# Gated attention with two MLP blocks on one core: lighter attention for the first batch, five weight pieces staged at the start, the spatial gate evicted to SBUF

## The chip, the cores and the metric

The kernel runs on one core of one Trainium2 chip. The metric is the time of one execution in device microseconds (us); lower is better. Beside the plain times there is one execution recorded by the hardware profiler, with every instruction of every engine.

## What is computed

Three blocks follow each other for 4 batches of 768 tokens with width 384 (8 heads of 48). First a linear attention with a decay per channel:

```
for t in range(S):
    state = alpha[:, :, t, :, None] * state + np.einsum('bhd,bhe->bhde', k[:, :, t], v[:, :, t])
    y[:, :, t] = np.einsum('bhd,bhde->bhe', q[:, :, t], state)
```

Then two MLP blocks, each added to its input:

```
xn = (x - mu) / np.sqrt(var + 1e-06) * g_ln
ch = np.maximum(xn @ w_ch1, 0.0) @ w_ch2
...
h = x @ w_in                                  # then a tanh gelu
u, v = (h[..., :d_ff // 2], h[..., d_ff // 2:])
v_n = (v - mu) / np.sqrt(var + 1e-06) * g_ln
v_s = np.einsum('ts,bsd->btd', w_sg, v_n) + b_sg[None, :, None]
gated = u * v_s
return (x + gated @ w_out).astype(np.float32)
```

## The kernel before

**Tiles and stages.** The tokens are cut into 24 chunks of 128, six to a batch; attention goes chunk by chunk, with a state carried from one to the next. Two chunks make a group, of which there are 12. The MLP work of a group comes in units, one PSUM tile each: A is the first matmul of the channel MLP (tile `pg`, L633), B its second (L667), C the input matmul of the spatial MLP (`pgv` L707, `pgu` L732). Once per batch follow six D units, the spatial gate (`pgs`, L752), and six E units, the output matmul (`pgo`, L781). A single matrix product is made of three fp16 products, of a high and a low half of each factor, so every result is evicted twice: ScalarE writes the high half, VectorE (or GpSimd) the low half as the difference. The tiles `pg`, `pgv`, `pgu`, `pgs` and `pgo` share three PSUM buffers (tag "g").

**Attention of the first batch.** `whole = i < NF` marks the chunks 0 to 5. They are computed in fp32: alpha, q and k are transposed on TensorE (`pt`, L283), the products of the decays are eight scans on VectorE (`F` forward, `K` backward, L342), `F` is multiplied by q and `K` by k (L311). `kh` is `K` scaled by `rf`, one over the decay of the whole chunk, in four ScalarE instructions (L398), `ks` its transposed form (L406), `vs` a copy of v (L491). Scores go to `sc` (L436), are masked into `ss` (L444), and `psy` (L530, L536) is the chunk's result. Each chunk also has an input check: three squares summed on ScalarE (L500) and one maximum on VectorE (L502) into `st_in`. Chunks 6 to 23 work on fp16 halves, made by DMA transposes, and keep their own path. In the order of instructions and in the rows, `wk` stands for `F`, `K`, `ks`, `kh` and `ss` of chunks 1 and 3, which borrow another buffer.

**Weights.** The weights arrive as float64 words. A piece of 0.786 MB is loaded by SyncE's queue (SP) into one of three `stage` buffers, narrowed by one ScalarE instruction (`bits`, L129) and two VectorE instructions (L131, L133), and split into halves (L139 to L143, with TensorE, or L146 and L147). There are six pieces of w1, six of w2, and then w_in, w_sg and w_out. A list `ready` keeps the loads in order; each step of it narrows one piece and issues the load of the next.

**Order.** A table of times (`LATE, TC, D0, ...`) sets the order in which the steps are written; a scheduler then places every instruction in the in-order queue of its engine, by its own model of time. An engine executes its queue strictly in that order, and so does SP's queue, which issues all DMAs.

## Time and profile before

| | |
|---|---|
| median of 3 runs | 701.03 us (700.08 to 703.02) |
| the profiled execution's own time | 702.77 us |
| its span, first to last instruction | 701.0 us |
| TensorE (PE) busy | 650.6 us, 93% of the span |
| VectorE (DVE) | 465.3 us, 66% |
| ScalarE (ACT) | 435.5 us, 62% |
| GpSimd (POOL) | 181.0 us, 26% |

The profiled execution took 1.77 us more than its span, and 1.74 us more than the median of the plain runs. Shares are averages over stages of different kinds: the start of the kernel, while weights are still coming in, is not limited by the same engine as the middle.

### The profile page before, as it was taken

How to read it: one execution, taken by the hardware profiler on the slowest of the kernel's cores; microseconds unless marked ns; L12 is line 12 of the kernel's file. 1: busy time of each engine (PE TensorE's matmuls, PEld its weight loads, DVE VectorE, ACT ScalarE, POOL GpSimd, SP SyncE). 2: the span in 40 equal slices, each digit the busy share in tenths (PEclk: the TensorE clock that was granted, in tenths of full speed). 3: DMA queues.
4: the chain of work that ended last, by engine and by line, in shares of the span. 5: the costliest groups of instructions: out<-in, count | busy, mean ns of one | idle time of the engine just before them, and what ended most of it. 6: DMA issues, size and time to landing. Idle time of an engine off the chain costs nothing.

```text
span 701.0 us, 14486 instructions
## 1 busy us (share of the span) xinstructions
PE 650.6 (93%) x5658; PEld 489.4 (70%) x5658; DVE 465.3 (66%) x911; ACT 435.5 (62%) x871; POOL 181.0 (26%) x413
## 2 busy tenths in 40 slices
PE   5889998979999988989999978998989989999996
PEld 3757776767776875667777866676656877676783
DVE  7999675867476795557745896559655678333464
ACT  5887646676878488488755688488652656322230
POOL 2121101423516220433532220432404311201100
PEclk9999999999999999999999999999999999999999
DMA  9996679765475149367382159275140612110102
GB/s 227 226 260 167 204 178 169 155 113 95 91 121 80 28 86 190 84 108 116 59 115 56 30 100 183 76 127 85 40 86 15 88 34 58 34 24 12 36 1 72
DMA packets 228637, 70.64 MB, mean 101 GB/s; under 512 B 219472, under 2 KB 222544, under 8 KB 228560
## 3 DMA queue, kind: packets, MB, share of 16 engines
q1 hardware_dynamic: 228560, 69.63, 52.0%
q8 instruction: 46, 0.75, 0.5%
q14 instruction: 31, 0.25, 0.1%
HBM read 35.79 MB, written 4.72 MB: 58 GB/s over the span
## 4 chain that ended last, share of the span: by engine, by line
PE 43%; DVE 17%; ACT 17%; DMA 13%; issue 5%; POOL 3%; SPq 1%; ACTq 0%; DVEq 0%; POOLq 0%
PE pg L667 13%; PE pg L633 9%; PE pgs L752 6%; DMA stage<-stage 4%; PE pgu L732 4%; PE pgv L707 4%; PE pgo L781 3%; ACT stage L306 3%; DMA wgs<-wsp 2%; ACT junk L500 2%; ACT stage L290 2%; DMA inp<-in_alpha_dram 2%; DVE F L345 2%; DVE sc L449 2%; DMA inp<-in_q_dram 2%
## 5 line engine op out<-in xcount | busy, mean ns | idle before, releaser
L633 PE MATMUL pg<-xhT,w1s 128*128 128x256 f16 (+1 forms) x1404 | 151.5, 267 | 13.2 <-DVE hT L639 6.1
L633 PEld LDWEIGHTS <-w1s 128*128 128x128 f16 x1404 | 128.4, 99 | 31.2 <-issue 14.9
L667 PE MATMUL pg<-w2s,hT 128*128 128x384 f16 x864 | 143.7, 326 | 0.3 <-ACT vg L710 0.3
L667 PEld LDWEIGHTS <-hT 128*128 128x128 f16 x864 | 83.9, 98 | 54.3 <-issue 0.2
L752 PE MATMUL pgs<-wgs,vn 128*128 128x256 f16 x864 | 96.1, 273 | 1.5 <-ACT junk L766 1.5
L752 PEld LDWEIGHTS <-vn 128*128 128x128 f16 x864 | 84.0, 98 | 12.0 <-issue 1.7
L639 DVE SCALAR_TENSOR_TENSOR hT<-pg,hT 128x512 f16<-128x512 f32 (+1 forms) x74 | 49.3, 672 | 46.8 <-ACT hT L638 46.6
L306 ACT ACTIVATE stage<-stage 128x1024 uint16<-128x1024 uint16 x48 | 64.7, 1354 | 19.1 <-DMA stage<-stage 19.0
L290 ACT ACTIVATE stage<-inp 128x1024 uint16<-128x1024 uint16 x48 | 50.1, 1053 | 30.3 <-DVE K L345 18.4
L150 POOL TENSOR_TENSOR kh<-K,kh 128x512 f16<-128x512 f32 x17 | 20.4, 1199 | 129.2 <-ACT kh L414 129.2
L732 PE MATMUL pgu<-x2T,wis 128*128 128x256 f16 x432 | 50.7, 274 | 1.6 <-DVE hT L639 1.3
L707 PE MATMUL pgv<-wis,x2T 128*128 128x512 f16 x216 | 49.9, 381 | 1.5 <-DVE hT L639 1.2
L781 PE MATMUL pgo<-wos,uT 128*128 128x384 f16 x288 | 48.3, 326 | 1.2 <-DVE x L783 1.2
L732 PEld LDWEIGHTS <-wis 128*128 128x128 f16 x432 | 41.7, 98 | 9.1 <-DVE hT L639 2.2
L638 ACT ACTIVATE hT<-pg 128x512 f16<-128x512 f32 (+1 forms) x74 | 42.0, 577 | 9.7 <-PE pg L633 9.6
L500 ACT ACTIVATE junk<-inp 128x384 bf16<-128x384 f32 x72 | 37.2, 519 | 8.0 <-DMA inp<-in_q_dram 4.0
L781 PEld LDWEIGHTS <-uT 128*128 128x128 f16 x288 | 28.0, 98 | 19.9 <-issue 2.0
L150 POOL TENSOR_TENSOR qs<-F,qs 128x512 f16<-128x512 f32 x18 | 20.6, 1143 | 79.7 <-ACT qs L386 79.7
L707 PEld LDWEIGHTS <-x2T 128*128 128x128 f16 x216 | 20.9, 99 | 24.4 <-issue 2.1
L468 ACT ACTIVATE ss<-sc 128x512 f16<-128x512 f32 x36 | 21.1, 596 | 19.0 <-DVE sc L449 19.0
L759 DVE SCALAR_TENSOR_TENSOR pgs<-pgs,g2c,bbc 128x256 f32<-128x256 f32 x48 | 23.4, 487 | 11.3 <-PE pgs L752 10.6
L716 DVE TENSOR_SCALAR vg<-vg,mvv,rv 128x512 f32<-128x512 f32 x24 | 13.8, 579 | 24.4 <-POOL rv L246 23.9
(172 smaller groups left out, 1100.8 us busy)
## 6 DMA issues: line engine op xcount, KB each, us to landing
stage<-in_moe_w_ch_dram SPq DMA_DIRECT2D x24, 384.0 KB, 5.2
inp<-in_alpha_dram SPq DMA_DIRECT2D x24, 192.0 KB, 3.3
inp<-in_q_dram SPq DMA_DIRECT2D x24, 192.0 KB, 4.1
inp<-in_k_dram SPq DMA_DIRECT2D x24, 192.0 KB, 4.4
inp<-in_v_dram SPq DMA_DIRECT2D x24, 192.0 KB, 4.4
out_dram<-x SPq DMA_DIRECT2D x24, 192.0 KB, 2.4
stage<-in_moe_w_in_dram SPq DMA_DIRECT2D x4, 768.0 KB, 4.3
stage<-in_moe_w_sg_dram SPq DMA_DIRECT2D x6, 384.0 KB, 3.4
```

The lines of the kernel that those rows point to most:

```text
L150: (nc.vector if on_dve else nc.gpsimd).tensor_tensor(out=out, in0=in0, in1=in1, op=ALU.subtract)
L290: nc.scalar.activation(out=sp, in_=t[:, n].rearrange("p h d -> p (h d)").bitcast(U16) .rearrange("p (x w) -> p w x", w=2), func=AF.Copy)
L306: nc.scalar.activation(out=words[:, :, :, gap:], in_=tr, func=AF.Copy)
L500: nc.scalar.activation(out=junk()[:, 0:DM].rearrange("p (h d) -> p h d", h=H), in_=t[:, n, :, 0:D], func=AF.Square, accum_out=st_in[:, i, ...
L633: nc.tensor.matmul(out=pg[:, f, :], lhsT=w1s[:, a, kk, ff * P:(ff + 1) * P], rhs=xhT[j][:, r, kk, o], start=(n_ == 0), stop=(n_ == 3 * KD ...
L638: nc.scalar.activation(out=hi, in_=src, func=AF.Relu)
L639: last_dve[0] = nc.vector.scalar_tensor_tensor(out=lo, in0=src, scalar=0.0, in1=hi, op0=ALU.max, op1=ALU.subtract)
L667: nc.tensor.matmul(out=box[s], lhsT=hidden(a, f, s), rhs=w2s[:, r, f, :], start=(f == 0 and a == 0 and r == 0), stop=(f == KF - 1 and r == 1))
L707: nc.tensor.matmul(out=pg, lhsT=x2T[j][:, a, kk, o], rhs=wis[:, r, kk, DG:DI], start=(n_ == 0), stop=(n_ == 3 * KD - 1))
L732: nc.tensor.matmul(out=pg[:, f, :], lhsT=wis[:, a, kk, ff * P:(ff + 1) * P], rhs=x2T[j][:, r, kk, 0:N], start=(n_ == 0), stop=(n_ == 3 * K ...
L752: nc.tensor.matmul(out=pg[:, f, :], lhsT=vn[b * NCH + s][:, a, d * P:(d + 1) * P], rhs=wgs[th][:, r, s, :], start=(n_ == 0), stop=(n_ == 3 ...
L781: nc.tensor.matmul(out=pg, lhsT=gt[key][:, d // 2, a, d % 2, o], rhs=wos[:, r, d, :], start=(d == 0 and a == 0 and r == 0), stop=(d == KG ...
```

## The change

Five edits come together.

1. The first batch's chunks lose their input checks, their copy `vs` (v is read where it was loaded) and the four scalings into `kh`. In their place the backward scans come first, the chunk's decay is taken from them, and the forward scans start at one over that decay instead of at a constant, so that `F` carries the scaling. Four small VectorE instructions replace two. The scale of v moves into the mask and into the update of the state.
2. The state is decayed (GpSimd) ahead of `psy` instead of after it.
3. The first two weight pieces are staged in the two `hT` buffers, which nothing uses yet, so five pieces can be loaded before one is narrowed; five loads are outstanding instead of six.
4. The tiny load `g1c` goes ahead of the first chunk's inputs.
5. A D unit is evicted from PSUM by its two VectorE instructions into an SBUF tile `tm` (two buffers); the multiplication by u and the low half go from VectorE to GpSimd, and ScalarE reads `tm`.

```diff
+        if n_loads[0] <= 2: ring.tile([P, 1536], I32, tag="hT", bufs=2, name="stage")
...
+        def decay_state():
+            nc.gpsimd.tensor_tensor(out=state, in0=state, op=ALU.mult,
+                                    in1=st_fe[:, i, :].unsqueeze(2).to_broadcast([P, NP, 2 * D]))
...
-                decays(T["F"][:, p, :], T["a"][:, p, :], S_Q)
+        if whole:
+            @step
+            def _():
+                fe = st_fe[:, i, :]
+                r = T["rf"] = p2.tile([P, NP], F32, tag="rf", name="rf")
+                nc.vector.scalar_tensor_tensor(out=r, in0=T["K"][:, :, 0:1]..., in1=T["a"][:, :, 0:1]...)
+                nc.vector.tensor_scalar(out=fe, in0=r, scalar1=2.0 ** -101, scalar2=None, op0=ALU.max)
+                nc.vector.tensor_scalar(out=r, in0=fe, scalar1=1.0 / S_Q, scalar2=None, op0=ALU.mult)
+                nc.vector.reciprocal(out=r, in_=r)
+            for p in range(NP):
+                @step
+                def _(p=p):
+                    scan_F(p, T["rf"][:, p:p + 1])
...
-                for p in range(NP):
-                    nc.scalar.activation(out=T["kh"][:, p, :], in_=T["K"][:, p, :], func=AF.Copy,
-                                         scale=T["rf"][:, p:p + 1])
...
-                T["Kr"] = T["kh"]
+                T["Kr"] = T["K"]
...
-                nc.vector.tensor_tensor(out=m, in0=T["sc", e], in1=causal..., op=ALU.mult)
+                nc.vector.scalar_tensor_tensor(out=m, in0=T["sc", e], scalar=S_V, op0=ALU.mult, op1=ALU.mult,
+                                               in1=causal.unsqueeze(1).to_broadcast([P, NP, P]))
...
-                nc.scalar.activation(out=T["vs"], in_=t[:, 2, :, 0:D], func=AF.Copy, scale=S_V)
+        if whole:
+            T["vs"] = t[:, 2, :, 0:D]
...
-                    in_psum = b >= KG_
-                    tm = pg if in_psum else p1.tile([P, 2, U], F32, tag="tm", name="tm")
+                    tm = p2.tile([P, 2, U], F32, tag="tm", name="tm")
...
-                    nc.vector.tensor_tensor(out=tm, in0=tm, in1=uT[key][:, o, :], op=ALU.mult)
+                    nc.gpsimd.tensor_tensor(out=tm, in0=tm, in1=uT[key][:, o, :], op=ALU.mult)
                     nc.scalar.activation(out=gt[key][:, dp, 0], in_=tm, func=AF.Copy)
-                    low(in_psum, gt[key][:, dp, 1], tm, gt[key][:, dp, 0])
+                    nc.gpsimd.tensor_tensor(out=gt[key][:, dp, 1], in0=tm, in1=gt[key][:, dp, 0], op=ALU.subtract)
...
+        nc.sync.dma_start(out=g1c, in_=g1.rearrange("(k p) -> p k", p=P))
         load_chunk(0)
-        nc.sync.dma_start(out=g1c, in_=g1.rearrange("(k p) -> p k", p=P))
...
         load_chunk(1)
-        for _ in range(3):
+        for _ in range(2):
             wload()
```

The table of times is unchanged; the scheduler places the instructions anew. Three places matter.

The first is SP's queue at the start, which issues the loads (`inp_94` and `inp_95` are the two input buffers, `stage` from `w_ch` a half of a weight piece). Before:

```order
L231 DMA inp_94<-in_v_dram 128x8x48
L847 DMA g1c<-in_moe_g_ln_dram 128x3x1
L162 DMA stage<-in_moe_w_ch_dram 128x768 x6
L231 DMA inp_95<-in_alpha_dram 128x8x48
...
L231 DMA inp_95<-in_v_dram 128x8x48
L878 DMA g2c<-in_moe_g_ln_dram 128x4x1
L880 DMA bbc<-in_moe_b_sg_dram 128x768
L231 DMA inp_94<-in_alpha_dram 128x8x48
...
L231 DMA inp_94<-in_v_dram 128x8x48
L162 DMA stage<-in_moe_w_ch_dram 128x768 x2
```

Now:

```order
L889 DMA g1c<-in_moe_g_ln_dram 128x3x1
L236 DMA inp_94<-in_alpha_dram 128x8x48
...
L236 DMA inp_94<-in_v_dram 128x8x48
L167 DMA stage<-in_moe_w_ch_dram 128x768 x6
L236 DMA inp_95<-in_alpha_dram 128x8x48
...
L236 DMA inp_95<-in_v_dram 128x8x48
L167 DMA stage<-in_moe_w_ch_dram 128x768 x4
L921 DMA g2c<-in_moe_g_ln_dram 128x4x1
L923 DMA bbc<-in_moe_b_sg_dram 128x768
L236 DMA inp_94<-in_alpha_dram 128x8x48
```

The fourth and fifth weight piece moved ahead of the third chunk's inputs, and `g1c` ahead of the first chunk's.

The second is VectorE's queue where the first unit of the first group A is evicted (`hT<-pg`). Before:

```order
L370 TENSOR_SCALAR st_fe<-F 128x4
L586 SCALAR_TENSOR_TENSOR xsp<-psy,st_mv,xsp 128x384
L444 TENSOR_TENSOR wk<-sc,causal 128x512 x2
L373 RECIPROCAL rf<-st_fe 128x4
L311 TENSOR_TENSOR F<-pt,F 128x4x128
L502 TENSOR_REDUCE st_in<-inp_94 128x1
L567 TENSOR_TENSOR state<-psd,state 64x4x48 x2
L639 SCALAR_TENSOR_TENSOR hT<-pg,hT 128x384
```

Now:

```order
L316 TENSOR_TENSOR F<-pt,F 128x4x128
L316 TENSOR_TENSOR K<-pt,K 128x4x128
L474 SCALAR_TENSOR_TENSOR ss_856<-sc,causal 128x512
L474 SCALAR_TENSOR_TENSOR ss_857<-sc,causal 128x512
L351 SCALAR_TENSOR_TENSOR wk<-pt,consts 128x127 x4
L601 SCALAR_TENSOR_TENSOR state<-psd,state 64x4x48 x2
L378 SCALAR_TENSOR_TENSOR rf<-wk,pt 128x4
L381 TENSOR_SCALAR st_fe<-rf 128x4
L681 SCALAR_TENSOR_TENSOR hT<-pg,hT 128x384
```

(Rows of weight pieces in between are left out of both.) Before, the masks of chunk 3 (`wk<-sc`) and all scans of chunk 4 stood ahead of the first eviction; now only chunk 2's masks and chunk 3's backward scans do.

The third is GpSimd's queue at the first batch's D units. Before, it held only the attention's work there:

```order
L150 TENSOR_TENSOR kh<-K,kh 128x512
L304 MEMSET stage 128x5
L150 TENSOR_TENSOR qs<-F,qs 128x512
L573 TENSOR_TENSOR sp<-state,sp 128x384
L241 TENSOR_SCALAR ve<-st_mv 128x1
L559 TENSOR_TENSOR state<-state,st_fe 128x384
```

Now:

```order
L803 TENSOR_TENSOR tm<-tm,uT 128x512
L155 TENSOR_TENSOR qs<-F,qs 128x512
L615 TENSOR_TENSOR sp<-state,sp 128x384
L246 TENSOR_SCALAR ve<-st_mv 128x1
L805 TENSOR_TENSOR uT<-tm,uT 128x512
L345 TENSOR_TENSOR state<-state,st_fe 128x384
```

The two GpSimd instructions of each D unit (L803 and L805) are interleaved with the attention's, and one of them now stands ahead of `qs`.

## Rows read from the trace of the kernel before

**Rows 1.** The profile's page: span, and busy us of each engine.
```profile
span 701.0 us, 14486 instructions
PE 650.6 (93%) x5658; PEld 489.4 (70%) x5658; DVE 465.3 (66%) x911; ACT 435.5 (62%) x871; POOL 181.0 (26%) x413
```

**Rows 2.** Windows: stretch, length, busy us of PE, PEld, DVE, ACT, POOL; clock, DMA.
```profile
0.00:62.00 62.00, 49.26 (x313) 35.97 (x314) 54.18 (x127) 45.58 (x102) 14.47 (x41) 1.00 1.12 236
62.00:101.00 39.00, 39.00 (x394) 30.30 (x392) 29.01 (x53) 24.21 (x50) 2.81 (x8) 1.00 0.56 179
100.00:165.00 65.00, 57.66 (x474) 44.93 (x473) 42.87 (x86) 44.69 (x90) 18.69 (x40) 0.95 0.80 141
222.00:252.00 30.00, 30.00 (x344) 26.60 (x343) 21.04 (x40) 17.92 (x32) 6.97 (x14) 1.00 0.31 55
252.00:300.00 48.00, 42.66 (x363) 29.96 (x360) 31.16 (x57) 35.81 (x75) 12.69 (x31) 1.00 0.67 121
```

**Rows 3.** What PE waited for: us in total, times, longest.
```profile
PE pg L633 <- DVE hT L639: 6.1, 5, 2.5
PE pg L633 <- ACT junk L766: 5.4, 4, 1.9
PE pgs L752 <- ACT junk L766: 1.5, 1, 1.5
```

**Rows 4.** Groups of ACT by form, 0 to 130 us: busy, mean ns, idle before.
```profile
L500 ACT ACTIVATE junk<-inp 128x384 bf16<-128x384 f32 x18 | 9.3, 518 | 7.0 <-DMA inp<-in_q_dram 4.0 <-DMA wgs<-wsp 1.9 <-DMA inp<-in_k_dram 1.0
L398 ACT ACTIVATE kh<-K,rf 128x128 f32<-128x128 f32 x16 | 5.1, 398 | 2.1 <-DVE K L311 1.8 <-DVE st_mv L581 0.3
L500 ACT ACTIVATION_READ_ACCUMULATOR junk<-inp 128x1 f32 x18 | 3.4, 191 | 0.0
L491 ACT ACTIVATE vs<-inp 128x384 f32<-128x384 f32 x6 | 3.1, 510 | 0.6 <-DMA inp<-in_v_dram 0.6
L398 ACT ACTIVATE wk<-wk,rf 128x128 f32<-128x128 f32 x8 | 2.6, 397 | 0.0
```

**Rows 5.** What DVE and ACT waited for, 0 to 110 us.
```profile
DVE stage L131 <- ACT bits L129: 5.9, 7, 2.2
ACT bits L129 <- DMA stage<-in_moe_w_ch_dram: 4.9, 5, 2.2
```

**Rows 6.** Timeline of DVE: start, us, instruction, idle before.
```profile
7.82 0.14 DVE L370 TENSOR_SCALAR st_fe<-F 128x4 f32<-128x4 f32 x1
12.45 0.96 DVE L131 SCALAR_TENSOR_TENSOR stage<-stage,bits 128x768 int32<-128x768 int32 x1 [2.23 <-ACT bits L129]
23.44 0.55 DVE L502 TENSOR_REDUCE st_in<-inp 128x1 f32<-128x384 f32 x1
40.94 2.61 DVE L342 TENSOR_TENSOR_SCAN wk<-pt,consts 128x128 f32<-128x128 f32 x8
100.93 0.69 DVE L639 SCALAR_TENSOR_TENSOR hT<-pg,hT 128x512 f16<-128x512 f32 x1 [1.44 <-ACT hT L638]
```

**Rows 7.** Timeline of SP's queue: start, us, load.
```profile
3.55 1.13 SPq L847 DMA_DIRECT2D g1c<-in_moe_g_ln_dram  x1
```

**Rows 8.** Tile `pgs` and line L150: ns min/median/max, first to last start.
```profile
L759 DVE SCALAR_TENSOR_TENSOR pgs<-pgs,g2c,bbc x48: 472/492/494, 227.5 to 684.1; 128x256 f32<-128x256 f32 x48
L762 DVE TENSOR_TENSOR pgs<-pgs,uT x24: 690/700/700, 229.2 to 684.6; 128x512 f32<-128x512 f32 x24
L150 DVE TENSOR_TENSOR uT<-pgs,uT x24: 652/691/693, 231.7 to 686.0; 128x512 f16<-128x512 f32 x24
L150 POOL TENSOR_TENSOR vn<-vg,vn x19: 1151/1156/1547, 127.6 to 605.6; 128x512 f16<-128x512 f32 x19
```

**Rows 9.** Timeline after the first batch's last D unit.
```profile
252.95 0.47 DVE L759 SCALAR_TENSOR_TENSOR pgs<-pgs,g2c,bbc 128x256 f32<-128x256 f32 x1
254.79 0.58 ACT L766 ACTIVATE junk<-pgs 128x512 bf16<-128x512 f32 x1
```

**Rows 10.** The later chunks' forward scan on DVE: ns min/median/max.
```profile
L345 DVE TENSOR_TENSOR_SCAN F<-stage,reset x16: 1219/1224/1871, 167.5 to 570.1; 128x516 f32<-128x516 f32 x16
```

More of the change, by code (lines that the diff above doesn't have):

```diff
@@ L115, in stage_tile @@
         return ring.tile([P, 1536], I32, tag="stage", bufs=NST, name="stage")
+    n_loads = [0]
     def stage_load():
-        return stage_tile().rearrange("p (f w) -> p f w", w=2)
+        n_loads[0] += 1
+        t = ring.tile([P, 1536], I32, tag="hT", bufs=2, name="stage") if n_loads[0] <= 2 else stage_tile()
+        return t.rearrange("p (f w) -> p f w", w=2)
     low_bits = []
@@ L368, in _ @@
         def _():
+            if whole:
+                T["q"] = transposed(0)
+                return
             fe = st_fe[:, i, :]
@@ L380, in _ @@
             if whole:
-                work(["ks", "kh"], F16)
-                for n in ("ks", "kh"):
-                    T[n] = T[n].rearrange("p a n t -> p (a n t)").bitcast(F32).rearrange("p (n t) -> p n t", n=NP)
+                work(["ks"], F16)
+                T["ks"] = T["ks"].rearrange("p a n t -> p (a n t)").bitcast(F32).rearrange("p (n t) -> p n t", n=NP)
             else:
@@ L506, in _ @@
         def _():
+            if whole and c:
+                decay_state()
             psd = ps.tile([P, NP, 2 * D], F32, tag="t", bufs=2, name="psd")
@@ L521, in _ @@
                     first = False
+        if whole:
+            stats_step[i] = len(steps)
         @step
@@ L557, in _ @@
             if c < NCH - 1:
-                if c:
-                    nc.gpsimd.tensor_tensor(out=state, in0=state, op=ALU.mult,
-                                            in1=st_fe[:, i, :].unsqueeze(2).to_broadcast([P, NP, 2 * D]))
+                if c and not whole:
+                    decay_state()
                 for e in range(2):
@@ L563, in _ @@
                     m = slice(D * e, D * e + D)
-                    if c == 0:
+                    if whole and c:
+                        nc.vector.scalar_tensor_tensor(out=state[o, :, m], in0=T["psd"][o, :, m], scalar=S_V,
+                                                       in1=state[o, :, m], op0=ALU.mult, op1=ALU.add)
+                    elif whole:
+                        nc.vector.tensor_scalar(out=state[o, :, m], in0=T["psd"][o, :, m], scalar1=S_V, scalar2=None,
+                                                op0=ALU.mult)
+                    elif c == 0:
                         nc.vector.tensor_copy(out=state[o, :, m], in_=T["psd"][o, :, m])
```

45 lines of the change are left out of this document (26 added, 19 removed).

## The prediction

> **What bounds the kernel now.** I read the page first: the span is 701.0 us and TensorE is busy for 650.6 of it, so 50.4 us of TensorE's idle time is all that this change can win, unless it shortens TensorE's own work [rows 1]. It doesn't: the same matrix products remain. The windows say where that idle time lies [rows 2]. From 0 to 62 us TensorE works 49.26, so 12.7 us are open; VectorE works 54.18 there, ScalarE 45.58, and the DMA engines are full (share 1.12, 236 GB/s). From 62 to 101 TensorE has no gap at all. From 100 to 165 it idles 7.3, and the granted clock is 0.95 of the full 2.4 GHz, the lowest of these stretches. While the first batch's D units run (222 to 252) it has no gap either, and right behind them (252 to 300) it idles 5.3.
>
> The waits say for whom TensorE stands still [rows 3]. The A units' first matmuls (L633) wait 6.1 us for VectorE's `hT`, which is a PSUM buffer that comes free late, and 5.4 us for ScalarE's `junk` (L766), the last reader of a D unit's buffer; the D units themselves wait 1.5 us for the same. So two things are paid for: the ramp, where VectorE is late with evictions, and the three D stages that another batch follows, where the buffer is held too long.
>
> **The change, part by part.** The sum is made against the profiled execution's own time, 702.8 us; the median of the runs is 1.74 us lower.
>
> *ScalarE in the ramp.* It loses 18 squares (9.3) and their 18 accumulator reads (3.4), the scalings `kh` (5.1 and 2.6) and `vs` (3.1): 23.5 us [rows 4], most of it before 101 us. That is no gain by itself, since TensorE's waits of the ramp name VectorE. It counts where ScalarE holds VectorE up: 5.9 us on `bits`, of which ScalarE in turn spent 4.9 waiting for the piece to land [rows 5]. Only the difference, about 1 us, is ScalarE's own lateness.
>
> *VectorE in the ramp.* Six maxima of 0.55 go, 3.3 us; four small instructions of about 0.14 replace two in each of six chunks, 1.7 us more; net 1.6 us less [rows 6]. The other edits only change the form: the masks become a scalar_tensor_tensor that reads PSUM, and the state update another. The masks have no row in the new form; the nearest is `hT` at L639, also read from PSUM with 512 columns, at 0.69 us, and 0.70 for the plain tensor_tensor of that width [rows 6, 8]. I price them at nothing, with 1 us either way for twelve masks.
>
> *VectorE's order.* This is the larger part. The first unit of the first group A is now written before chunk 4's eight scans (2.61 us in one row of the timeline), chunk 3's masks and some statistics: about 10 us of VectorE's work stood ahead of that eviction and is behind it now [rows 6]. But ahead of the second group's first `hT` (100.93 us before [rows 6]) stands as much as before, less the 1.6. The 10 us are borrowed. They become a gain only as far as VectorE's own idle time is filled: it has 7.8 us of that up to 62, and 10.0 from there to 101 [rows 2]. Bounds: nothing, if VectorE's inputs still come at the same time (TensorE, which feeds it, has no gap from 62 to 101), and 8, about half of the 17.8 and most of TensorE's 12.7. I take **4**, nearer to the lower bound than to all of the idle time, as TensorE's waits on `hT` total 6.1 and not all of them lie here.
>
> *Five pieces at once, and `g1c`.* The fourth and fifth piece now pass chunk 2's inputs in SP's queue. The DMA engines are full, so two pieces of 0.786 MB at 236 GB/s push those inputs back by 6.7 us [rows 2], while ScalarE's wait for pieces is 4.9 in all [rows 5]: what the one wins the other may lose. Chunk 2's transposes are late if its inputs are. Net nothing; bounds 3 either way (a wait on pieces or a wait on chunk 2, whichever of VectorE's two sources is late next). `g1c` costs SP 1.13 us ahead of chunk 0's alpha [rows 7], at worst a loss of 1.1 at the very start. Against it stands that VectorE waited 2.23 us at 12.45 for the first `bits` [rows 6], which ScalarE, now without squares, can give sooner. Net nothing.
>
> *100 to 165 us.* The rest of the 23.5 us of ScalarE and the last of the borrowed order fall here, where ScalarE works 44.69 of 65 and VectorE 42.87 [rows 2]: neither is full. I take **1**, between 0 and 3 (3.3 is what the missing 5% of clock in 65 us is worth).
>
> *The D units.* VectorE loses 24 x (0.70 + 0.69) = 33 us. GpSimd gains 48 instructions; its nearest row is a subtraction of the same 128x512 at 1.156 us, between 1.151 and 1.547 [rows 8], so 55 us, 74 at the upper end. A unit thus gives it 2.31 us. The first batch's units follow each other every 5.1 us (first eviction 227.5, last 252.95, five steps [rows 8, 9]), and GpSimd's 6.97 busy us of 30 become 20.8 [rows 2]: it keeps up, if what it needs is there. What is bought is the buffer. Before, it came free when ScalarE's square was done, 254.79 + 0.58 = 255.37 for the last unit. Now it is free when the second eviction instruction has ended, 252.95 + 0.47 = 253.42, 2 us sooner [rows 9]. Three D stages are followed by other work, and the waits on `junk` are 5.4 + 1.5 = 6.9 us in all [rows 3]. VectorE's backlog adds to `hT`'s 6.1, of which I count half for these stages. Bounds: 2 (only the D-to-D waits and a part of the others) and 9 (6.9 plus most of 3). I take **5**, below 6.9, since a buffer that is free sooner hands part of the wait to VectorE, which is next in line. At the very end, where E needs the last low half, GpSimd is 2 x 1.156 - 1.39 = 0.9 us later than VectorE was: at most 0.9 lost.
>
> The page of the Trainium skill that bears on this speaks against the edit: the GPSIMD Engine Reference, section "Engine selection", sends elementwise work with two inputs to VectorE and calls GpSimd about twice as slow. This trace has 1.156 against 0.69 us, a ratio of 1.67. By the page's ratio the new work would be 48 x 1.39 = 67 us, 2.8 per unit; that is still under 5.1, so the sum is the same by either, and the page's warning counts for the third rival below. Its section "Specifications" adds that the two engines share SBUF interfaces. The row that bears on it here is the later chunks' forward scan, 1.224 us in the median and 1.871 at most [rows 10]; no row shows what ran beside it caused that.
>
> *Sum.* 4 + 1 + 5 = 10: 702.8 - 10 = 692.8 of a profiled execution, and 1.74 less, **691**, for the median.
>
> **Rivals.**
>
> *More than that.* VectorE's idle time in the ramp is filled to its bound (8), all waits of the D stages go (9), and the clock stays full from 100 to 165 (3, of 3.3). For it: ScalarE loses half of its 45.58 us of work in the ramp, and VectorE's waits on ScalarE chain on. Against it: TensorE had no gap from 62 to 101, so what it starts sooner must find its inputs sooner. 8 + 9 + 3 = 20, about 681; I centre it at 683. 0.22.
>
> *Given back.* The ramp is bound by VectorE's 54.18 of 62 us and by the DMA queue, and the 10 us are repaid at the second group: nothing. The D stages' waits become waits for `hT`, and 3 are left of the 5: 702.8 - 3 - 1.74 = 698, with 2 either way. For it: ahead of the second group's `hT` as much stands as before. 0.16.
>
> *Slower.* GpSimd's queue is strictly in order, and `qs`, `sp` and the state's decay of the next batch now stand between its two instructions of a D unit. The first of these waits for VectorE's evictions, which wait for a unit of TensorE. So an attention step can be late by the 2.31 us of a unit's work, and so can what TensorE does with it. With two chunks beside each of three D stages and the lateness once per chunk, two of these instructions each, that is 2 x 3 x 2.31 = 13.8 us against 10 won: 702.8 + 3.8 - 1.74 = 705. The point from which it decides is 10 / 6 = 1.7 us per chunk. For it: GpSimd goes from a quarter to two thirds of the stage. Against it: the attention's steps there are written well ahead of the chunk's end. 0.10.
>
> **How the numbers follow.** The forecast, 687 to 697, has 0.52: its lower end is the ramp's 6 with the D stages' 7 and the 1, its upper end 0 to 1 of the ramp with the D stages' 3 to 4. With 0.22 below, 0.16 at 698 and 0.10 at 705 these make 1. The range must leave out no more than 0.2: from 681, which cuts a little of the first rival (0.06), to 700, which leaves out the third and a little of the second (0.12). A measurement of this kernel can tell about 0.5%, 3.5 us, from no change, so faster is below 697.5: all of the forecast, the first rival, and a little of "given back", less a little of the forecast's upper end, 0.74. The same, up to 704.5, is the rest of "given back" and a part of the slower case's low end, 0.17. Slower has 0.09.
>
> **What would show it.** In the changed kernel's profile, TensorE should be idle some 4 us less in its first 62 to 101 us, the waits of L675 on `hT` should be nearer 2 than 6.1, and the waits on `junk` should be gone, as ScalarE no longer reads the buffer. GpSimd should be busy near 236 us and VectorE near 431. If chunk 2's inputs land late, VectorE or TensorE will name `inp` or `pt` in the first 40 us. If GpSimd is late, TensorE or ScalarE in the D stages will name `qs`, `sp` or `state`. The forecast is wrong if the scans or evictions on VectorE become much longer beside GpSimd's new work, if the two `tm` buffers fill (VectorE then names GpSimd's L805), or if the ramp's idle time only moves to the second group.

## The result and the profile after

The changed kernel takes 697.67 us (median of 8 runs, 695.06 to 699.68). The kernel before, run beside it, took 702.9 (8 runs), so the ratio is 0.9925, 95% interval 0.9904 to 0.9946: 5.3 us faster, where the forecast was about 10. The profiled execution took 697.87 us.

The page of the changed kernel, span and busy time, answers to [rows 1]:

```profile
span 696.1 us, 14452 instructions
PE 653.8 (94%) x5658; PEld 492.2 (71%) x5658; DVE 441.1 (63%) x870; ACT 416.6 (60%) x805; POOL 242.4 (35%) x462
```

TensorE idles 696.1 - 653.8 = 42.3 us, against 50.4. That is 8.1 us less, near the forecast's 10; but the same 5658 matmuls are busy 3.2 us longer, so only 4.9 us of the span are gone. Cut at the first D unit (223.4 us before, 221.7 after) and at the last matmul of E, the windows show where the 8.1 us were. Before:

```profile
0.00:223.40 223.40, 202.83 (x1661) 151.07 (x1662) 165.64 (x339) 157.37 (x318) 61.77 (x140) 0.98 0.78 161
223.40:694.90 471.50, 447.43 (x3999) 338.29 (x3997) 299.05 (x572) 278.14 (x554) 119.20 (x274) 1.00 0.41 73
```

After:

```profile
0.00:221.70 221.70, 202.84 (x1661) 151.68 (x1662) 167.74 (x346) 138.57 (x252) 59.96 (x142) 0.98 0.79 162
221.70:689.80 468.10, 450.59 (x3998) 340.52 (x3997) 272.72 (x524) 278.07 (x554) 182.49 (x322) 0.99 0.41 73
```

Ahead of the first D unit, the stretch called the ramp here, TensorE idles 18.9 us instead of 20.6; behind it, 17.5 instead of 24.1. The longer busy time lies behind it too.

The windows answer to [rows 2] (same stretches and columns):

```profile
0.00:62.00 62.00, 50.89 (x360) 37.32 (x361) 53.36 (x118) 38.05 (x67) 12.07 (x35) 1.00 1.07 236
62.00:101.00 39.00, 37.80 (x344) 29.44 (x342) 32.35 (x69) 18.19 (x32) 4.95 (x15) 1.00 0.83 204
100.00:165.00 65.00, 58.72 (x495) 45.92 (x493) 44.61 (x96) 40.15 (x76) 17.36 (x41) 0.95 0.70 132
222.00:252.00 30.00, 30.00 (x349) 27.03 (x347) 16.79 (x34) 18.53 (x38) 17.60 (x21) 1.00 0.35 57
252.00:300.00 48.00, 44.34 (x377) 30.52 (x375) 30.34 (x56) 35.93 (x72) 16.84 (x35) 0.96 0.69 123
```

Up to 101 us TensorE idles 12.3 us (11.1 + 1.2), and before 12.7. From 252 to 300 it idles 3.7 instead of 5.3, but the granted clock there is 0.96 and was 1.00.

What TensorE waited for (us in total, times, longest), beside [rows 3]:

```profile
PE pg L675 <- DVE hT L681: 9.1, 7, 2.6
PE pgo L822 <- DVE hT L681: 3.4, 3, 2.0
PE psd L546 <- ACT ks L436: 3.4, 1, 3.4
PE pgu L774 <- DVE hT L681: 0.9, 2, 0.5
```

The kernel before had two more rows on `hT`:

```profile
PE pgu L732 <- DVE hT L639: 1.3, 2, 0.8
PE pgv L707 <- DVE hT L639: 1.2, 2, 0.7
```

The waits on `junk` (6.9) are gone. The waits on `hT` grew from 8.6 in all to 13.4, and one long wait on `ks` is new.

Where the two places stand is told by the first and last start of a line's matmuls, for the A units (up to 300 us) and the first batch's D units. In the kernel before:

```profile
L633 PE MATMUL pg<-xhT,w1s x648: 217/272/418, 61.6 to 268.4; 128*128 128x256 f16 x108, 128*128 128x128 f16 x54
L752 PE MATMUL pgs<-wgs,vn x216: 270/273/282, 223.4 to 249.7; 128*128 128x256 f16 x108
```

In the changed kernel:

```profile
L675 PE MATMUL pg<-xhT,w1s x648: 217/272/283, 51.4 to 265.3; 128*128 128x256 f16 x108, 128*128 128x128 f16 x54
L794 PE MATMUL pgs<-wgs,vn x216: 269/273/282, 221.7 to 247.9; 128*128 128x256 f16 x108
```

The first group starts 10.2 us sooner; the first D unit only 1.7.

### The profile page after: what moved, and what is told of

Read it like the earlier page. It is cut to its first block, busy times and chain, and to the rows that moved or that the text cites. A ratio compares the mean times of both kernels' runs of the same rounds, so it can differ in the third digit from the quotient of the medians.

```text
span 696.1 us, 14452 instructions
## 1 busy us (share of the span) xinstructions
PE 653.8 (94%) x5658; PEld 492.2 (71%) x5658; DVE 441.1 (63%) x870; ACT 416.6 (60%) x805; POOL 242.4 (35%) x462
## 4 chain that ended last, share of the span: by engine, by line
PE 42%; DVE 21%; ACT 18%; DMA 11%; issue 4%; POOL 4%; SPq 1%; ACTq 0%; DVEq 0%
PE pg L709 11%; PE pg L675 7%; PE pgs L794 6%; PE pgo L822 5%; DMA stage<-stage 4%; PE pgv L749 4%; ACT stage L311 3%; PE pgu L774 3%; DMA inp<-in_alpha_dram 3%; ACT stage L295 2%; ACT junk L532 2%; DVE F L354 2%; DMA inp<-in_q_dram 2%; DVE sc L479 2%; DVE K L354 2%
## 5 line engine op out<-in xcount | busy, mean ns | idle before, releaser
L675 PE MATMUL pg<-xhT,w1s 128*128 128x256 f16 (+1 forms) x1404 | 152.5, 268 | 9.9 <-DVE hT L681 9.1
L675 PEld LDWEIGHTS <-w1s 128*128 128x128 f16 x1404 | 128.9, 99 | 28.5 <-issue 10.6
L311 ACT ACTIVATE stage<-stage 128x1024 uint16<-128x1024 uint16 x48 | 64.8, 1355 | 18.2 <-DMA stage<-stage 17.8
L822 PE MATMUL pgo<-wos,uT 128*128 128x384 f16 x288 | 50.2, 333 | 3.4 <-DVE hT L681 3.4
L749 PE MATMUL pgv<-wis,x2T 128*128 128x512 f16 x216 | 50.4, 384 | 0.1
L774 PEld LDWEIGHTS <-wis 128*128 128x128 f16 x432 | 42.3, 100 | 8.7 <-DVE hT L681 1.3
L800 DVE SCALAR_TENSOR_TENSOR tm<-pgs,g2c,bbc 128x256 f32<-128x256 f32 x48 | 20.9, 477 | 39.7 <-PE pgs L794 31.1
L822 PEld LDWEIGHTS <-uT 128*128 128x128 f16 x288 | 28.4, 100 | 22.8 <-issue 5.7
L155 POOL TENSOR_TENSOR qs<-F,qs 128x512 f16<-128x512 f32 x18 | 20.6, 1146 | 66.2 <-ACT qs L422 66.2
L246 POOL TENSOR_SCALAR ve<-mvv 128x1 f32<-128x1 f32 x24 | 5.3, 222 | 97.1 <-DVE mvv L756 95.9
L803 POOL TENSOR_TENSOR tm<-tm,uT 128x512 f32<-128x512 f32 x24 | 32.4, 1348 | 18.2 <-DVE tm L800 18.1
L804 ACT ACTIVATE uT<-tm 128x512 f16<-128x512 f32 x24 | 14.9, 623 | 36.1 <-POOL tm L803 36.1
```

Of the source, the lines that this page charges most:

```text
L155: (nc.vector if on_dve else nc.gpsimd).tensor_tensor(out=out, in0=in0, in1=in1, op=ALU.subtract)
L311: nc.scalar.activation(out=words[:, :, :, gap:], in_=tr, func=AF.Copy)
L675: nc.tensor.matmul(out=pg[:, f, :], lhsT=w1s[:, a, kk, ff * P:(ff + 1) * P], rhs=xhT[j][:, r, kk, o], start=(n_ == 0), stop=(n_ == 3 * KD ...
L749: nc.tensor.matmul(out=pg, lhsT=x2T[j][:, a, kk, o], rhs=wis[:, r, kk, DG:DI], start=(n_ == 0), stop=(n_ == 3 * KD - 1))
L774: nc.tensor.matmul(out=pg[:, f, :], lhsT=wis[:, a, kk, ff * P:(ff + 1) * P], rhs=x2T[j][:, r, kk, 0:N], start=(n_ == 0), stop=(n_ == 3 * K ...
L803: nc.gpsimd.tensor_tensor(out=tm, in0=tm, in1=uT[key][:, o, :], op=ALU.mult)
```

## The experiments

Each was compared with the kernel before on the same chip, in five rounds; its ratio is to that kernel, with a 95% interval. In each expectation, "theory" is the reading held likelier and "rival" the other. "First D unit" is the first start of the `pgs` matmuls in the profiled execution (223.4 before, 221.7 changed). It scatters: five complete kernels with all the ramp's edits (the changed one, `no_d`, `d_sbuf_dve`, `checks_dve`, `ks_dve`) have it between 221.0 and 223.8, so a difference of up to 3 us says nothing by itself. In `att_only` it is at 223.6, in `att_d` at 226.0 and in `stage_only` at 230.0, the last in the slowest of that kernel's 12 runs.

**The change in its parts.** `d_only` is the kernel before with edit 5 alone, `att_only` with edits 1 and 2, `stage_only` with 3 and 4, `no_d` with 1 to 4. The core of `d_only`'s edit:

```diff
-                    nc.vector.tensor_tensor(out=tm, in0=tm, in1=uT[key][:, o, :], op=ALU.mult)
+                    nc.gpsimd.tensor_tensor(out=tm, in0=tm, in1=uT[key][:, o, :], op=ALU.mult)
...
-                    low(in_psum, gt[key][:, dp, 1], tm, gt[key][:, dp, 0])
+                    nc.gpsimd.tensor_tensor(out=gt[key][:, dp, 1], in0=tm, in1=gt[key][:, dp, 0], op=ALU.subtract)
```

Expected of `d_only`:

> The kernel before with the D units' edit alone (eviction into tm by VectorE, multiplication and low half on GpSimd, tm with two buffers). Theory: TensorE's waits on junk (6.9 us before) go, a part comes back as waits on hT, idle falls by 4 to 6 us from 50.4, and the clock falls at one or two more places, which takes 1 to 3 us back: 2 to 4 us faster than before, ratio 0.994 to 0.997. Rival: the whole gain of the change (ratio 0.9925) is this edit's, 0.992 to 0.993, and the ramp's edits are worth nothing. Second rival: waits only change their name, 0.999 to 1.001.

Measured: 0.9932 (0.9911 to 0.9952). That is the first rival's range: the D edit alone gives nearly all of the change's gain. Its first D unit is at 223.9; the gain comes behind it. From there to E's last matmul, `d_only` takes 465.4 us and the kernel before 471.5. TensorE's idle time in that stretch parts the kernels more clearly than one length does: 22.1 to 24.6 us in the five kernels that keep a D unit in PSUM (before, `att_only`, `stage_only`, `no_d`, `no_wgs_before`), and 16.3 to 21.0 in the nine that evict it early and whose checks of chunks 6 to 23 are as in the changed kernel (some of these runs follow below).

Expected of `att_only`:

> The kernel before with the first batch's lighter attention alone (no checks, no copy of v, no scalings into kh, scans in the new order), six pieces staged as before, D units as before. Theory: VectorE has the same amount of work ahead of the second group's hT, so the earlier start of the first group is repaid: at most 2 us faster, ratio 0.997 to 1.000. Rival: the 23.5 us less of ScalarE's work is what made the changed kernel faster: 4 us or more, under 0.995.

Measured: 0.9987 (0.9974 to 1.0001). The lighter work of ScalarE, 23.5 us by the prediction's rows and 18.1 by its busy time (435.5 to 417.4; an accumulator's read overlaps its square), is worth about 1 us, 2 at most.

Expected of `stage_only`:

> The kernel before with five loads outstanding in five buffers, and g1c first; nothing else. Theory: nothing, 0.998 to 1.002, since DMA is full in the first 62 us and what a piece wins chunk 2's inputs lose. Rival: the weights were what the ramp waited for (ScalarE's 4.9 us on them): 3 us or more, under 0.996.

Measured: 1.0016 (1.0002 to 1.0029), no gain, which fits the DMA engines' share of 1.12 in [rows 2].

Expected of `no_d`:

> The changed kernel with the D units as they were (PSUM until the square is done, multiplication and low half on VectorE). Theory: keeps only the ramp's share, about 1.5 us: 0.996 to 0.999 of before, with TensorE idle some 49 us and first D unit at about 222 us, and the junk waits of 5 to 7 us back. Rival: the ramp's edits made the 5 us, 0.992 to 0.994.

Measured: 0.9972 (0.9954 to 0.999), 2 us, as the theory had it. In its trace the A units and the D units stand so:

```profile
L675 PE MATMUL pg<-xhT,w1s x648: 217/272/283, 51.3 to 267.9; 128*128 128x256 f16 x108, 128*128 128x128 f16 x54
L794 PE MATMUL pgs<-wgs,vn x216: 269/273/283, 222.9 to 249.2; 128*128 128x256 f16 x108
```

Ten us of lead at the first group again, and half a us of it left at the first D unit.

**The early start without the staging edit.** `att_d` has edits 1, 2 and 5.

```diff
-        if n_loads[0] <= 2: ring.tile([P, 1536], I32, tag="hT", bufs=2, name="stage")
...
-        for _ in range(2):
+        for _ in range(3):
             wload()
```

> The changed kernel without the staging edit and with g1c behind chunk 0's inputs, so the lighter attention and the D edit alone. The staging edit alone measured 1.0016. Theory: it is worth nothing or a little loss also here: 0.990 to 0.993 of before. Rival: it needs the lighter attention to pay (five pieces at once let the first group start at 51 us rather than 57), and without it 0.994 to 0.997.

Measured: 0.9932 (0.9909 to 0.9954). Staging and `g1c` don't matter here either.

**The D edit in two.** `d_sbuf_dve` leaves PSUM as early as the changed kernel, but VectorE multiplies and subtracts, in SBUF:

```diff
-                    nc.gpsimd.tensor_tensor(out=tm, in0=tm, in1=uT[key][:, o, :], op=ALU.mult)
+                    nc.vector.tensor_tensor(out=tm, in0=tm, in1=uT[key][:, o, :], op=ALU.mult)
```

(the subtraction likewise).

> The changed kernel with the multiplication and the low half of the D units back on VectorE, reading and writing the SBUF tile tm; PSUM is left as early as in the changed kernel. It parts the D edit in two. Theory: the early release of PSUM is what pays, so this one keeps most: 0.992 to 0.996, no waits on junk. Rival: it is VectorE's 33 us less that pay (hT comes sooner); then most of the D edit's gain goes: 0.996 to 0.999, and TensorE's waits on hT grow by several us.

Measured: 0.9925 (0.9895 to 0.9954), the changed kernel's own ratio. VectorE works 464.7 us in it, against 441.1 in the changed kernel. So the early release of the PSUM buffer pays; taking work from VectorE adds nothing that five rounds can tell.

GpSimd was not free of cost in the changed kernel either. In the third batch's D stage, both `tm` buffers are full, and VectorE waits for GpSimd to empty one, twice, while GpSimd waits for ScalarE's half:

```profile
553.64 1.16 POOL L805 TENSOR_TENSOR uT<-tm,uT 128x512 f16<-128x512 f32 x1 [2.30 <-ACT uT L804]
554.83 0.88 DVE L800 SCALAR_TENSOR_TENSOR tm<-pgs,g2c,bbc 128x256 f32<-128x256 f32 x2 [5.04 <-POOL uT L805]
559.28 0.88 DVE L800 SCALAR_TENSOR_TENSOR tm<-pgs,g2c,bbc 128x256 f32<-128x256 f32 x2 [3.57 <-POOL uT L805]
561.27 2.20 DVE L354 TENSOR_TENSOR_SCAN F<-stage,reset 128x516 f32<-128x516 f32 x1
562.34 2.19 POOL L803 TENSOR_TENSOR tm<-tm,uT 128x512 f32<-128x512 f32 x1
563.39 2.23 DVE L354 TENSOR_TENSOR_SCAN K<-stage,reset 128x516 f32<-128x516 f32 x1
564.56 0.63 ACT L804 ACTIVATE uT<-tm 128x512 f16<-128x512 f32 x1 [2.80 <-POOL tm L803]
566.34 0.20 PE L588 MATMUL psy<-vs,ss 128*128 128x48 f16 x1 [1.56 <-ACT ss L498]
569.11 0.98 PE L588 MATMUL psy<-vs,ss 128*128 128x48 f16 x20 [1.62 <-DVE ss L155]
```

VectorE's scans come behind these waits, and beside GpSimd's multiplication they take 2.2 us, where the median is 1.2; the multiplication takes 2.19, where its median is 1.27. ScalarE waits 2.80 us for that multiplication and evicts `ss` behind it. TensorE then waits 3.9 us on `ss` in three pieces (1.56, 0.70 and 1.62); in `d_only` the same three make 4.2, in `d_sbuf_dve` there are two of 1.39 and 0.42. So the work on GpSimd costs some 2 us of waits here; whether that is what it wins elsewhere, so that the two kernels measure the same, is not shown.

**ScalarE behind a D stage.** The changed kernel's ScalarE behind the first batch's last D unit, by start, length and idle time before it:

```profile
255.23 0.62 ACT L804 ACTIVATE uT<-tm 128x512 f16<-128x512 f32 x1
255.75 0.62 ACT L807 ACTIVATE junk<-tm 128x512 bf16<-128x512 f32 x1
256.27 0.19 ACT L807 ACTIVATION_READ_ACCUMULATOR junk<-tm 128x1 f32 x1
256.37 0.51 ACT L732 ACTIVATE junk<-x 128x384 bf16<-128x384 f32 x1
256.78 0.19 ACT L732 ACTIVATION_READ_ACCUMULATOR junk<-x 128x1 f32 x1
256.87 0.58 ACT L680 ACTIVATE hT<-pg 128x512 f16<-128x512 f32 x1
```

VectorE and TensorE there:

```profile
257.49 0.69 DVE L681 SCALAR_TENSOR_TENSOR hT<-pg,hT 128x512 f16<-128x512 f32 x1 [1.21 <-ACT hT L680]
258.23 2.13 PE L675 MATMUL pg<-xhT,w1s 128*128 128x256 f16 x18 [1.04 <-DVE hT L681]
267.51 12.89 PE L822 MATMUL pgo<-wos,uT 128*128 128x384 f16 x68 [1.96 <-DVE hT L681]
```

TensorE waits for VectorE's half of `hT`, VectorE for ScalarE's half, and ScalarE comes to it only after the last D unit's copy and square and one more square (L732). The buffer that came free sooner was filled by the next A unit, whose eviction stands in the same queue. `no_checks` takes load from that queue: it leaves the input checks of chunks 6 to 23 out.

```diff
-            @step
-            def _():
-                stats()
```

> The changed kernel without the input checks (three squares on ScalarE, one maximum on VectorE) of the chunks 6 to 23 as well; it leaves these checks out, as the changed kernel does for the chunks 0 to 5. Theory: behind a D stage TensorE waits on hT because ScalarE's queue is full (squares, copies for the transposes) and its hT copy comes late, so 38 us less of ScalarE's work take away a good part of the waits on hT (9.1 + 3.4 us) and some clock dips: 4 to 7 us faster than the changed kernel, 0.983 to 0.988 of before. Rival: these waits come from VectorE or GpSimd, or ScalarE's place in the order decides and not its load: within 2 us of the changed kernel, 0.990 to 0.994.

Measured: 0.9861 (0.9823 to 0.99), first D unit at 223.7. ScalarE works 392.0 us, VectorE 430.8 (the maxima are gone too), and TensorE idles 41.1. The theory's ratio, though the waits of L671 on `hT` are still 8.6 us. Of the 4.8 us of span that are gone against the changed kernel, 1.2 are idle time and 3.6 busy time of the same matmuls, at a clock of 0.989 instead of 0.984. What is shown is that this load costs time; that the gain comes by `hT` is not, nor which of the two engines it comes from. `checks_dve` computes the checks' squares on VectorE instead:

```diff
-                nc.scalar.activation(out=junk()[:, 0:DM]..., in_=t[:, n, :, 0:D],
-                                     func=AF.Square, accum_out=st_in[:, i, n:n + 1])
+                nc.vector.scalar_tensor_tensor(out=junk()[:, 0:DM]..., in0=t[:, n, :, 0:D], scalar=1.0,
+                                     in1=t[:, n, :, 0:D], op0=ALU.mult, op1=ALU.mult, accum_out=st_in[:, i, n:n + 1])
```

> The changed kernel with the squares of the input checks of chunks 6 to 23 on VectorE (three scalar_tensor_tensor with accumulated sums per chunk) in place of ScalarE; all checks are computed. Theory: behind D it is ScalarE's load that counts, and VectorE has room since the D edit; 54 squares of about 0.6 us are 35 us for VectorE, which then works as long as before the change. Most of the 4.5 us that leaving the checks out gave stays: 0.986 to 0.990 of before. Rival: VectorE writes the last half of hT, its new work comes ahead of that as ScalarE's did, and nothing is won or up to 4 us lost: 0.992 to 0.998.

Measured: 0.9923 (0.9894 to 0.9952), the rival: nothing won. VectorE works 469.9 us, and TensorE waits 10.8 us on `hT` at L675 and 5.0 at L822. So moving the squares off ScalarE is not enough: on VectorE, which writes the other half of `hT`, they cost about as much.

**The clock.** In windows of 1 us, the kernel before shows three stretches of some 3.4 us at the lower level (0.5 of 2.4 GHz, 1.2 GHz), ahead of its end, and the changed kernel five, one of them twice as long. Each comes right behind one of TensorE's long waits: 2.01, 2.16 and 2.53 us before; 3.42, 1.96, 2.60, 2.42, and 1.56, 0.70 and 1.62 shortly one after the other, after the change. Not every long wait is followed by one: those of 2.54 and 2.70 us in the first 10 us of the changed kernel are not, nor is one of 1.91 us on `junk` in the kernel before (at 411.76). Windows of the changed kernel around the first:

```profile
117.00:122.00 5.00, 4.87 (x46) 3.59 (x44) 2.44 (x4) 1.08 (x1) 0.64 (x2) 1.00 1.28 197
122.00:125.00 3.00, 0.00 (x0) 0.00 (x0) 2.12 (x3) 2.52 (x4) 1.54 (x5) 0.97 0.60 50
125.00:131.00 6.00, 5.70 (x26) 4.65 (x27) 3.75 (x8) 5.29 (x12) 2.30 (x7) 0.50 0.70 134
```

After 3 us without a matmul, TensorE is busy for 6 us at half the clock. Over the 8 runs of the changed kernel the clock lies between 0.978 and 0.989 and the spans between 697.8 and 693.2, with a correlation of -0.95. In other kernels time and clock go together less: -0.63 over the 92 runs of the kernel before beside the experiments, 0.07 over the 12 of `no_d`. TensorE's busy time does follow the clock: in the profiled executions of the 14 kernels with the same 5658 matmuls it goes from 649.1 us (`att_only`, clock 0.995) to 657.5 (`wgs_scalar`, 0.976), with a correlation of -0.95. The two profiled executions lie further apart than their kernels do: 0.992 before and 0.984 after, with medians of 0.989 over those 92 runs and 0.9845 over the 8. Two kernels put work into the wait at 122. `fill` has 24 fp32 matmuls in the `psd` tile, ahead of its own:

```diff
+            for n in range(24 if i == NF - 1 else 0):
+                nc.tensor.matmul(out=psd[:, n % NP, :], lhsT=ident, rhs=ident[:, 0:2 * D],
+                                 start=(n % NP == 0), stop=(n % NP == NP - 1), skip_group_check=True)
```

> The changed kernel with 24 more matmuls (fp32, 128x96, some 3.2 us at the full clock, of values that the next matmul overwrites) put into chunk 5's psd ahead of its own, where TensorE waits 3.4 us for ks. They add work and take no wait away. Theory: the granted clock falls because TensorE stood idle; filled, it stays full after 125 us, which is worth up to 3 us: 0.988 to 0.992 of before, PE busy without the fill (3.2) lower than 653.8. Rival: the low clock has nothing to do with this wait: the dip stays, or the time is the same or up to 3 us longer, 0.992 to 0.997.

Measured: 1.0043 (1.0018 to 1.0068). It was no test: the added matmuls waited 3.39 us for the same eviction, and then took 8.41 us, in 48 passes, at a mean clock of 0.65 (130 to 138 us). `fill2` puts 12 into the scores, which come first:

```diff
+            for n in range(12 if i == NF - 1 else 0):
+                nc.tensor.matmul(out=T["sc", 0][:, n % NP, :], lhsT=T["K"][:, n % NP, :], rhs=T["F"][:, n % NP, :], start=True, stop=True)
```

> The changed kernel with 12 more fp32 matmuls of 128x128 (24 passes, some 3.5 us at the full clock) in chunk 5's scores, overwritten by the real ones, which come right ahead of TensorE's wait of 3.4 us for ks; they wait for nothing that comes later. Theory: the granted clock falls because TensorE stood idle there; the added work fills the idle time, the dip at 125 us is gone, and the 3 us of time that it cost pays for the added work: 0.989 to 0.993 of before. Rival: the clock falls there all the same (it goes by something else than the wait): the dip stays, 0.994 to 0.999.

Its windows:

```profile
122.00:125.00 3.00, 3.00 (x29) 2.92 (x28) 1.92 (x3) 0.36 (x1) 0.78 (x3) 1.00 1.45 172
125.00:131.00 6.00, 4.75 (x49) 4.24 (x48) 4.96 (x8) 5.38 (x8) 1.71 (x6) 1.00 0.62 113
```

The stretch of low clock is gone with that idle time. The kernel measured 0.9976 (0.9954 to 0.9998) all the same, since the masks came 2.8 us later and TensorE waited 2.59 for them (a wait that no low clock followed). That trace is also the fastest of the kernel's 12 runs (696.64 us, clock 0.994; the others have 0.98 to 0.989), and in it another stretch of some 3.4 us at the low clock begins at 99.8 us, ahead of which no wait from 85 us on was longer than 0.39. So one trace speaks for the theory, and has a stretch that speaks against it; that filling the wait saves time was not shown, and what makes the clock fall stays open.

**The wait on ks.** In ScalarE's queue the eviction of chunk 5's `ks` stands behind an instruction that waits for a later chunk's inputs (the expectations say chunk 7's; it is the ninth load of an alpha, so chunk 8's). `ks_dve` gives it to VectorE:

```diff
+                if i == NF - 1:
+                    nc.vector.tensor_copy(out=T["ks"], in_=pk)
```

> The changed kernel, with chunk 5's eviction of ks moved from ScalarE to VectorE. In the changed kernel this eviction stood in ScalarE's queue behind a copy of chunk 7's inputs that had just landed, and TensorE waited 3.4 us for it (3.8 us without the D edit), after which its granted clock was 0.5 for some 7 us. Theory: the ramp's lead is given back in waits of this kind between 101 and 222 us, and this is the largest: without it the first D unit starts 2 to 5 us sooner than 221.7, and the ratio to before is 0.985 to 0.990. Rival: another input (the weights of the spatial gate, x2T) is late next and takes the wait over: 0.991 to 0.994, first D unit at 221 or later.

Measured: 0.9907 (0.9873 to 0.9941), not to be told from the changed kernel; first D unit 221.0. TensorE's wait is the same:

```profile
PE psd L549 <- DVE ks L437: 3.3, 1, 3.3
```

VectorE's queue, too, has an instruction ahead of it that waits for those inputs (the maximum of the same chunk's check, which starts at 123.6). Both queues are held by one load; ahead of that, VectorE also waited 2.65 us for one of the transposes `wgs<-wsp`.

**The input side.** `no_wgs` leaves the twelve DMA transposes of the spatial gate's weights out (so that gate is computed from a constant):

```diff
-                    nc.sync.dma_start_transpose(out=wgs[i][:, a, :, n * P:(n + 1) * P], in_=sp[a])
+                    nc.sync.dma_start(out=wgs[i][0:1, a, 0, n * P:(n + 1) * P], in_=sp[a][0:1, 0:P])
```

> The changed kernel without the twelve DMA transposes of the spatial gate's weights (L221): GpSimd fills the tiles with a constant and two tiny DMAs stand in the transposes' place, so the spatial gate is not computed from its weights. TensorE's work is the same. Theory: the ramp's lead ends at the input side: between 100 and 125 us SP's queue (1.24 us per transpose and its waits) and the DMA engines (share 0.92) bring chunk 7's alpha late (issued 116.8, landed 122.4), and ScalarE and VectorE have an instruction that waits for it ahead of chunk 5's ks. Without the transposes that wait of 3.3 to 3.9 us goes and the first D unit starts 3 to 6 us before 221.7: 0.984 to 0.989 of before. Rival: the ramp is bound by VectorE's and ScalarE's work, which stays: D unit at 220.5 to 222, 0.990 to 0.994.

Measured: 0.9865 (0.9831 to 0.9898), first D unit at 219.0, and in its trace no wait on `ks` is left. That would speak for the theory, had the kernel before not gained as much by the same edit, `no_wgs_before`:

> The kernel before without the twelve DMA transposes of the spatial gate's weights, replaced as in the run on the changed kernel (which starts its first D unit 2.7 us sooner by it, and measured 0.9865 against 0.9925); the spatial gate is not computed from its weights. Theory: the input side is where the changed kernel's lead ends, so the kernel before, which has no such lead, gains less: first D unit at 222.5 to 223.4, ratio 0.998 to 1.000. Rival: the transposes cost either kernel the same, and the lead is not repaid there: first D unit 2 to 3 us before 223.4, 0.993 to 0.996.

Measured: 0.995 (0.9933 to 0.9968), first D unit at 221.4: 2.0 us sooner than the kernel before has it, against 2.7, which the scatter doesn't part. The transposes cost either kernel some 3 to 4 us and are not where the lead went. `wgs_scalar` computes everything and has ScalarE issue them:

```diff
-                    nc.sync.dma_start_transpose(out=wgs[i][:, a, :, n * P:(n + 1) * P], in_=sp[a])
+                    nc.scalar.dma_start_transpose(out=wgs[i][:, a, :, n * P:(n + 1) * P], in_=sp[a])
```

> The changed kernel with the twelve transposes of the spatial gate's weights issued by ScalarE's queue in place of SyncE's; everything is computed. Without these transposes either kernel was 0.5 to 0.6% faster. Theory: what they cost is SP's in-order queue (their waits for wsp hold up chunk 6's and 7's inputs), and with another queue most of it is won: 0.986 to 0.990 of before, first D unit at 219 to 220.5. Rival: they cost the DMA engines' time, or ScalarE's queue holds them up the same way: 0.991 to 0.995, first D unit at 221 to 223.

Measured: 1.0136 (1.0106 to 1.0166), first D unit at 238.5. ScalarE's waits from 80 to 160 us:

```profile
ACT wsp L151 <- issue: 11.2, 2, 5.6
ACT wsp L151 <- DMA wgs<-wsp: 6.8, 2, 4.2
ACT bits L134 <- issue: 6.3, 1, 6.3
```

ScalarE stands still where it issues, up to 6.3 us, and all its evictions behind it. Of the two queues tried, SP's can better afford these waits.

**VectorE in the ramp.** `less_dve` leaves one of the two narrowing instructions out for 8 weight pieces, `less_dve_before` does so in the kernel before, and `less_both` drops the transposes too.

```diff
+        narrowed.append(0)
+        if len(narrowed) > 8:
             nc.vector.scalar_tensor_tensor(out=lo, in0=hi, scalar=-0x80000000, in1=lo, op0=ALU.bitwise_and,
```

> The changed kernel with one of the two narrowing instructions on VectorE left out for the first 8 weight pieces (the signs of these weights are lost): 8 x 0.95 = 7.6 us less of VectorE's work in the first 60 us. Theory: after the early start of the first group the rest is paced by inputs and order, so D starts at most 2 us before 221.7: 0.989 to 0.993 of before. Rival: VectorE's work paces the whole ramp, and most of the 7.6 us is won: D unit at 214 to 218, 0.981 to 0.987.

> The kernel before with the same 8 instructions left out. Theory: before the change the first group waited for VectorE, so it gains more here than in the changed kernel: 2 to 4 us, first D unit at 219 to 221.5, 0.994 to 0.997. Rival: neither kernel's ramp is paced by VectorE: D unit within 1 us of 223.4, 0.998 to 1.001.

> The changed kernel with both left out, the 8 narrowing instructions and the 12 transposes. Theory: the two limits stand one behind the other, so together they give more than the sum of each (2.7 us for the transposes and 0 to 2 for VectorE): first D unit at 213 to 217, 0.977 to 0.984. Rival: they add at most, D unit at 217 to 219.5, 0.984 to 0.988.

Without the weights' signs the kernel's own range checks send it into a second, slow computation, so the whole times (ratios 6.83, 6.85, 6.84) say nothing; the stretch up to the first D unit comes ahead of that and can be read. First D units: 224.9, 224.5 and 218.3. Less work of VectorE before 62 us (7.1 us less in the changed kernel, 9.6 in the kernel before) brings the first D unit forward in neither, and with the transposes gone, by 0.7. In `less_dve`, TensorE's idle time of 12.3 us up to 101 fell to 10.2, and that from 101 to 222, which was 6.6 in the changed kernel, rose to 10.5:

```profile
0.00:62.00 62.00, 51.94 (x350) 38.02 (x350) 46.29 (x113) 37.17 (x64) 12.64 (x41) 0.97 1.08 244
62.00:101.00 39.00, 38.89 (x366) 31.00 (x367) 29.28 (x53) 20.03 (x37) 4.30 (x7) 1.00 0.79 188
101.00:222.00 121.00, 110.54 (x931) 81.81 (x930) 83.12 (x168) 78.94 (x148) 42.24 (x91) 0.97 0.62 109
```

The granted clock of the first 62 us fell as well, to 0.97 here and to 0.92 in `less_dve_before`, from 1.00 in either kernel, so a part of the idle time that was saved can have gone into slower matmuls:

```profile
0.00:62.00 62.00, 51.89 (x321) 38.42 (x322) 44.63 (x109) 45.77 (x104) 12.23 (x40) 0.92 1.09 236
```

None of the complete kernels beats the changed one by more than the measurement can tell.

## Why the prediction was right in direction and too large

**The step that failed** is "VectorE's order", of which the prediction said "The 10 us are borrowed" and then took 4 for them, with 1 more from 100 to 165 us. The order did what it says: the first group starts 10.2 us sooner. But TensorE's idle time up to 101 us fell by 0.4, from 12.7 to 12.3, and from 100 to 165 by 1.1, from 7.3 to 6.3. VectorE's idle time up to 101 fell from 17.8 to 15.3, so 2.5 us of it were filled, and still TensorE idled as much. A unit that starts sooner only takes the place of other work; the ramp is paid for in TensorE's idle time, and that was not counted. `no_d` puts the worth of all the ramp's edits at 2 us (0.7 to 3.2), `att_only` at 1, `stage_only` at less than nothing. Beside the D edit they add nothing that a trace shows: TensorE idles 8.6 us less than before in `d_only`, which has none of them, and 8.1 less in the changed kernel. What paces TensorE from 101 to 222 us stays open: neither VectorE's work nor the transposes alone, as far as the runs tell, and the scatter of the first D unit hides smaller causes.

**The D term came out, by two errors that cancel.** It was 5, and `d_only` measured 4.8 (ratio 0.9932 of 702.25). But by its trace TensorE idles 8.6 us less than before, more than the 6.9 of `junk`, and is busy 3.1 longer, at a clock of 0.984: the waits saved were mis-sized low, and the clock's cost was missing. That the two made 5 is luck. The working holds in its main step: the buffer's release is what pays (`d_sbuf_dve`), and "hands part of the wait to VectorE, which is next in line" is what the waits on `hT` show, with ScalarE behind VectorE. GpSimd's price was as said: the multiplication, with two fp32 inputs, took 1.27 us in the median, the subtraction 1.16:

```profile
L803 POOL TENSOR_TENSOR tm<-tm,uT x24: 1261/1268/2192, 226.7 to 679.6; 128x512 f32<-128x512 f32 x24
L805 POOL TENSOR_TENSOR uT<-tm,uT x24: 1147/1157/1329, 230.4 to 681.6; 128x512 f16<-128x512 f32 x24
```

GpSimd is busy 242.4 us, not 236, and VectorE 441, not 431 (in `d_only` the later chunks' backward scans alone take 22.3 us for 19.3). "It keeps up, if what it needs is there" failed in the third D stage, where GpSimd had to wait for ScalarE: VectorE names L805 there for 8.6 us in all, which the prediction had set down as a sign of being wrong, and the scans became longer, which was another. None of TensorE's larger waits names GpSimd, but those on `ss` at 566 to 569 us stand behind it. Against VectorE's 0.70 [rows 8] the multiplication is 1.8 times as long. That is near the "~2× slower for 2-input ops" of the Trainium skill's GPSIMD Engine Reference, section "Engine selection". The measured total doesn't tell the edit on GpSimd from the same one on VectorE (0.9925 each).

**The clock was left out as a cost.** The prediction saw 3.3 us to win there and took none to lose. TensorE's busy time grew by 3.2 us at the same work, with five stretches at the lower level in place of three; so much for this pair of traces, whose clocks lie further apart than those of the plain runs. Behind the first D stage, waits of 0.88 and 1.30 on `junk` and 0.87 on `hT` became 1.04, 0.54 and 1.96 on `hT`, together no shorter, and the last was followed by 3.4 us at half the clock. From 252 to 300 us TensorE did only 14 matmuls more than before (377 and 363). By rows: 8.1 less idle, 3.2 more busy, 4.9 off the span.

**Other points.** Staging was worth nothing, as said. VectorE's 1.6 us less did not come (465.3 us before and in `no_d`). The slower rival (attention steps late by GpSimd's queue) came only in small, on `ss` in one D stage and not on `qs`, `sp` or `state`. "More than that" failed at the ramp. "Given back" named 698, and 697.67 came; it was near for the ramp (nothing, where 2 were measured) and low for the D stages (3, where `d_only` measured 4.8), so that its number came so close is partly luck. The parts, 2 and 4.8, make 6.8 where the whole measured 5.3; their intervals are wide enough for that.

## What to carry to other kernels

Count a reordering by the idle time of the engine that bounds the kernel, stretch by stretch, and not by how much sooner one unit starts. Before a buffer is freed earlier, look at what evicts the unit that takes it next: the gain ends at the first full in-order queue behind it, here ScalarE's behind the first D stage, and GpSimd's with ScalarE's in the third. And look at the granted clock behind the waits that remain: less idle time in fewer, longer waits won less here than its sum.
